# One transfer for w2 and one for dw2 in a decode block with its gradients: rows of 16.6 KB, one tile, a shared buffer for discarded results

## Chip, cores, metric

One Trainium2 chip, one core. The metric is the device time in microseconds of one execution, the median of several runs. Runs of two kernels are compared only when they were taken in the same rounds on the same chip.

## The reference, cut to what matters

The forward pass mixes an attention block with one query (A) and a small MLP (B) through a gate. The kernel computes the output and all gradients.

```python
g = sigmoid((x * gate_w).sum(-1))
a = A(x, k_cache, v_cache, wq, wo)     # 32 heads, 4096 keys, 128 wide: K and V are 33.6 MB each
b = B(x, w1, b1, w2)                   # h = x@w1 + b1; act = h*tanh(softplus(h)); act @ w2
out = g * a + (1 - g) * b
# outputs: out, dx, dK, dV, dwq, dwo, dw1, db1, dw2, dgate_w     (w2 is 1728 x 640, bf16)
```

K and V are read once and dK and dV are written once: 134 of the 165 MB that move. w2 is small beside this. Of its 1728 rows the first 1664 lie 13 to a partition: 13 x 640 x 2 B = 16640 B per partition.

## The kernel before

Heads are worked one after the other. In each, VectorE, PE and ScalarE pass small results to each other (row maximum, softmax, products); the two outer products dK and dV are VectorE's largest pieces. Loads go out on the sync queue (SP), most stores on GpSimd's (POOL). The MLP is cut into steps that are put into gaps ("slots") of the heads, at most four VectorE steps in a head.

```python
CH = [(0, 5), (5, 9), (9, FCN)]        # thirds of w2
def load_w2(c):
    a, b = CH[c][0], min(CH[c][1], FM)
    w2cs[c] = mlp.tile([P, 5, D], BF16, name="w2c", tag="w2c", bufs=2)     # two buffers for three thirds
    nc.sync.dma_start(w2cs[c][:, 0:b - a, :], w2_v[:, a:b, :])
...
load_k(2); load_v(2)
load_w2(0)
w2r = mlp.tile([FR, D], BF16, name="w2r", tag="w2r")
nc.sync.dma_start(w2r[:], B_w2[FB:F, :])
load_w2(1)
...
def dw2_part(c, f0, f1):               # dw2 is written in place over w2, then stored
    def f():
        for fc in range(f0, f1):
            r = rows(fc)
            nc.vector.tensor_scalar(w2p(fc), db_bc[0:r, :], m["act_f"][0:r, fc:fc + 1], None, ALU.mult)
        if f1 == CH[c][1]:
            a, b = CH[c][0], min(f1, FM)
            nc.gpsimd.dma_start(dw2_v[:, a:b, :], w2cs[c][:, 0:b - a, :])
...
# steps of third 2: four empty slots after the store of third 0, the load, eight empty slots, then its work
```

Steps `dh` (13 + 1 of them) and `dw2` belong to w2. `dxm` (10) and `dw1` (5) come after all `dh` steps. In each head the start is one instruction, the row maximum of the scores; I use it as the clock of the heads:

```python
def period(h):
    m32 = small.tile([P, 1], F32, name="m32", tag="m32")
    nc.vector.reduce_max(m32[:], S, axis=AX.X)
    ...
```

## Time and profile before

| | before |
|---|---|
| time, median of 3 runs | 402.32 us (402.15 to 402.79) |
| span of the profiled run | 400.8 us |
| bytes moved by DMA | 164.92 MB, 412 GB/s over the span |
| VectorE, PE busy | 76%, 75% |

A line of a stretch gives its length, the busy time of PE, weight load, VectorE, ScalarE and GpSimd with instruction counts, the granted clock, the share of time that the 16 DMA engines were busy (packets of two rings can overlap a little, so up to 1.03) and GB/s. The main reading of the page and the stretches is in the prediction below. Five further lines of the kernel before: from its chain of waits (start, length, what), the load of a K tile that compute waited for; from its stretches, the one that step 2 speaks of; from the view of the MLP tile, the steps after w2 (duration min/median/max, then first and last start); from the waits of the SP queue, a wait near the end (total us, times, longest):

```profile
49.57 33.56 DMA Kn<-in_A_k_cache_dram
```

```profile
168.00:174.00 6.00, 1.94 (x26) 1.10 (x25) 3.73 (x10) 0.58 (x1) 0.56 (x1) 0.71 1.02 421
```

```profile
L530 DVE SCALAR_TENSOR_TENSOR junk<-w_sb,dh_bc x10: 1040/1052/1059, 254.3 to 328.6; 128x864 bf16<-128x864 bf16 x10
L537 DVE TENSOR_SCALAR w_sb<-dh_bc,cols_f x5: 652/662/671, 274.1 to 332.4; 128x1728 bf16<-128x1728 bf16 x5
```

```profile
SPq L368 <- DMA out_dram<-dV_sb: 9.8, 1, 9.8
```

### The profile page before, as it was taken

To read this page: it belongs to the slowest core of one execution; us is meant where nothing else is said; L and a number is where in the kernel's file an instruction comes from. 1 tells how busy PE (TensorE), PEld (TensorE's weight loads), DVE (VectorE), ACT (ScalarE), POOL (GpSimd) and SP (SyncE) were. 2 spreads that over 40 slices of the span, in tenths; PEclk is the share of its full clock that TensorE was granted. 3 is DMA by queue.
4 is the path that set the end of the run, shared out by engine and by line. 5 is a ranking of instruction groups with operands and counts; after the bars stand their busy time and mean duration, and the time that the engine had idled before them with its cause. 6 is when DMAs were issued, how large, how long until landed. Compare 5 with 4: busy or idle time off the path is not lost.

```text
span 400.8 us, 13361 instructions
## 1 busy us (share of the span) xinstructions
PE 301.0 (75%) x5752; PEld 266.0 (66%) x5752; DVE 303.1 (76%) x783; ACT 178.2 (44%) x403; POOL 47.0 (12%) x94
## 2 busy tenths in 40 slices
PE   0788888678888788768879788838888888888300
PEld 0577888567777677658868778718777678877200
DVE  3339666556799999767658999836999997898860
ACT  1455454325545555326533555604545545555000
POOL 0001111021110111211110112101111121111000
PEclk9899999959999999969977999967999999999755
DMA  8999999999999999999999999999999999999995
GB/s 292 417 407 405 418 426 421 407 423 421 424 421 424 422 422 416 422 424 424 419 424 426 422 422 417 417 425 424 421 421 424 424 423 418 425 420 418 424 383 229
DMA packets 28359, 164.92 MB, mean 412 GB/s; under 512 B 3260, under 2 KB 3964, under 8 KB 12556
## 3 DMA queue, kind: packets, MB, share of 16 engines
q1 hardware_dynamic: 17136, 93.41, 56.5%
q0 software_dynamic: 11104, 70.64, 42.3%
q8 instruction: 45, 0.74, 0.7%
q14 instruction: 14, 0.11, 0.1%
q10 hardware_dynamic: 60, 0.01, 0.0%
HBM read 82.03 MB, written 82.03 MB: 409 GB/s over the span
## 4 chain that ended last, share of the span: by engine, by line
DVE 38%; DMA 32%; PE 20%; ACT 5%; issue 3%; ACTq 0%; SPq 0%
DMA Kn<-in_A_k_cache_dram 30%; DVE dK_sb L605 9%; DVE dV_sb L605 9%; PE tr L580 8%; DVE junk L378 5%; ACT tT L582 4%; DVE junk L278 3%; PE sA L660 3%; PE sA L589 3%; PE sB L713 3%; DVE junk L530 2%; DVE wo_g L367 1%; DMA vec_rows<-in_gate_w_dram 1%; DVE dj L700 1%; DVE dwq_t L732 1%
## 5 line engine op out<-in xcount | busy, mean ns | idle before, releaser
L582 ACT COPY tT<-tr 128x512 f32<-128x512 f32 x256 | 142.4, 587 | 127.8 <-PE tr L580 126.0
L589 PEld LDWEIGHTS <-tT 128*128 128x128 bf16 x2048 | 79.8, 98 | 40.3 <-ACT tT L582 34.6
L580 PE MATMUL tr<-ident_f,Kn 128*128 128x128 f32 x512 | 81.6, 297 | 9.2 <-DMA Kn<-in_A_k_cache_dram 9.2
L605 DVE TENSOR_TENSOR dV_sb<-p_bf,qd 128x2048 bf16<-128x2048 bf16 x64 | 78.0, 1218 | 0.2 <-issue 0.2
L605 DVE TENSOR_TENSOR dK_sb<-ds_bf,qd 128x2048 bf16<-128x2048 bf16 x64 | 77.7, 1216 | 0.0
L580 PE MATMUL tr<-ident_f,Vn 128*128 128x128 f32 x512 | 72.9, 278 | 0.0
L580 PEld LDWEIGHTS tr<-ident_f,Kn 128*128 128x128 f32 x512 | 61.0, 152 | 10.4 <-issue 10.4
L589 PE MATMUL sA<-qd,tT 128*128 128x48 bf16 x1024 | 48.7, 187 | 23.8 <-ACT dq_all L718 12.7
L580 PEld LDWEIGHTS tr<-ident_f,Vn 128*128 128x128 f32 x512 | 56.3, 142 | 0.0
L589 PE MATMUL sB<-qd,tT 128*128 128x48 bf16 x1024 | 46.0, 183 | 0.0
L660 PEld LDWEIGHTS <-Vn 128*128 128x128 bf16 x1024 | 30.2, 95 | 10.9 <-issue 10.9
L660 PE MATMUL sA<-e_bf,Vn 128*128 128x48 bf16 x1024 | 30.7, 183 | 8.1 <-DVE zs L680 6.5
L622 POOL DMA_DIRECT2D out_dram<-dK_sb x30 | 17.2, 574 | 138.9 <-DVE rz L682 86.5
L713 PE MATMUL sB<-ds_bf,Kn 128*128 128x48 bf16 x1024 | 32.2, 186 | 1.4 <-DVE ds_bf L702 1.4
L664 DVE TENSOR_REDUCE m<-sA 128x1 f32<-128x32 f32 x32 | 6.1, 189 | 32.9 <-PE sA L589 26.4
L713 PEld LDWEIGHTS <-Kn 128*128 128x128 bf16 x1024 | 29.5, 98 | 1.6 <-issue 1.6
L635 POOL DMA_DIRECT2D out_dram<-dV_sb x26 | 14.1, 542 | 135.8 <-DVE o_all L705 53.4
L278 DVE SCALAR_TENSOR_TENSOR junk<-wo_g,da_bc 128x640 bf16<-128x640 bf16 x32 | 26.2, 820 | 1.7 <-ACT da_bc L229 1.1
L378 DVE SCALAR_TENSOR_TENSOR junk<-wq_g,dq_bc 128x1024 bf16<-128x1024 bf16 (+1 forms) x25 | 25.1, 1005 | 0.2
L700 DVE TENSOR_SCALAR_CACHE_REDUCE dj<-sB,rz 128x128 f32<-128x128 f32 x32 | 11.1, 346 | 13.2 <-PE sB L694 13.2
L289 PE MATMUL q_ps<-wq_g,cols_bf 128*128 128x512 bf16 x40 | 13.1, 469 | 10.5 <-DMA wq_g<-in_A_wq_dram 10.5
L684 ACT ACTIVATE p_bf<-e_bf,rz 128x64 bf16<-128x64 bf16 x32 | 11.1, 348 | 13.9 <-DVE rz L682 11.1
(148 smaller groups left out, 268.8 us busy)
## 6 DMA issues: line engine op xcount, KB each, us to landing
Kn<-in_A_k_cache_dram SPq DMA_DIRECT2D x32, 1024.0 KB, 24.0
Vn<-in_A_v_cache_dram SPq DMA_DIRECT2D x32, 1024.0 KB, 28.0
out_dram<-dK_sb POOLq DMA_DIRECT2D x30, 1024.0 KB, 11.8
out_dram<-dV_sb POOLq DMA_DIRECT2D x26, 1024.0 KB, 11.8
wq_g<-in_A_wq_dram SPq DMA_DIRECT2D x4, 1280.0 KB, 23.2
wo_g<-in_A_wo_dram SPq DMA_DIRECT2D x8, 640.0 KB, 17.6
out_dram<-wo_g POOLq DMA_DIRECT2D x7, 640.0 KB, 11.8
out_dram<-dwq_t SPq DMA_DIRECT2D x4, 896.0 KB, 17.5
```

The lines of the kernel that those rows point to most:

```text
L278: nc.vector.scalar_tensor_tensor(junk[:, 0:D], in0=wos[g][:, i, :], scalar=1.0, in1=da_bc[:], op0=ALU.mult, op1=ALU.mult, accum_out=gp["do ...
L289: nc.tensor.matmul(q_ps[:], lhsT=x_bf[:, rc:rc + 1].to_broadcast([P, P]), rhs=wq[:, rc, off:off + GD], start=(rc == 0), stop=(rc == RC - 1))
L378: nc.vector.scalar_tensor_tensor(junk[:, c0:c1], in0=wqs[w][:, rc, c0:c1], scalar=1.0, in1=dq_bc[:, w * WG * Dh + c0:w * WG * Dh + c1], op ...
L580: nc.tensor.transpose(tp[:, t, :], flat[:, k * P:(k + 1) * P], ident_f[:])
L582: nc.scalar.copy(sb[:].rearrange("p a b -> p (a b)"), tp[:].rearrange("p a b -> p (a b)"))
L589: nc.tensor.matmul(out[:, 2 * k:2 * k + W], lhsT=tb[:, t, par, :], rhs=vec[:, par, :].unsqueeze(1).to_broadcast([P, W // 2, 2]), start=(pa ...
L605: nc.vector.tensor_tensor(dst[:, a:b, :].rearrange("p j (a b) -> p j a b", b=2), col[:, a:b, :].unsqueeze(2).to_broadcast([P, n, Dh // 2, 2]),
L622: ring(h).dma_start(dKv[h], st["dK"][:])
L635: ring(h).dma_start(dVv[h], st["dV"][:])
L660: nc.tensor.matmul(O, lhsT=vts[h][:, j, :], rhs=st["e"][:, j:j + 1].to_broadcast([P, W]), start=(j == 0), stop=(j == J - 1))
L700: nc.vector.tensor_scalar(dj[:], PT, rz[:], None, ALU.mult, ALU.add, accum_out=dd[:])
L713: nc.tensor.matmul(DQ, lhsT=kts[h][:, j, :], rhs=ds[:, j, 0:1].to_broadcast([P, W]), start=(j == 0), stop=(j == J - 1))
```

## The change

The intent is fewer and longer transfers for w2 and dw2, and no wait of the third chunk for a free buffer. w2 now has a tile of its own of 16640 B per partition in place of two buffers of 6400 B. Two discarded VectorE results (`pj`, `dj`) move into the junk buffer, so they need no tiles of their own (640 B per partition).

```diff
-    def load_w2(c):
-        a, b = CH[c][0], min(CH[c][1], FM)
-        w2cs[c] = mlp.tile([P, 5, D], BF16, name="w2c", tag="w2c", bufs=2)
-        nc.sync.dma_start(w2cs[c][:, 0:b - a, :], w2_v[:, a:b, :])
+    w2_all = mlp.tile([P, FM, D], BF16, name="w2_all", tag="w2_all")
+    for c in range(NCH):
+        w2cs[c] = w2_all[:, CH[c][0]:min(CH[c][1], FM), :]
 ...
-    load_w2(0)
+    nc.sync.dma_start(w2_all[:], w2_v)
     w2r = mlp.tile([FR, D], BF16, name="w2r", tag="w2r")
     nc.sync.dma_start(w2r[:], B_w2[FB:F, :])
-    load_w2(1)
 ...
-                    nc.gpsimd.dma_start(dw2_v[:, a:b, :], w2cs[c][:, 0:b - a, :])
                     if f1 == FCN:
+                        nc.gpsimd.dma_start(dw2_v, w2_all[:])
                         nc.gpsimd.dma_start(out_8[FB:F, :], w2r[:])
 ...
-            if c < 2:
-                done[f"w2_{c}"] = -1
-            else:
-                (4 empty steps, the load of the third chunk, 8 empty steps)
+            done[f"w2_{c}"] = -1
 ...
-        pj = small.tile([P, J], F32, name="pj", tag="pj", bufs=1)
+        pj = f32v(junk[:])[:, 0:J]
 ...
-        dj = small.tile([P, P], F32, name="dj", tag="dj", bufs=1)
+        dj = f32v(junk[:])[:, 0:P]
```

More of the change, by code (lines that the diff above doesn't have):

```diff
@@ L497, in f @@
                 if f1 == CH[c][1]:
-                    a, b = CH[c][0], min(f1, FM)
-                    nc.gpsimd.dma_start(dw2_v[:, a:b, :], w2cs[c][:, 0:b - a, :])
                     if f1 == FCN:
+                        nc.gpsimd.dma_start(dw2_v, w2_all[:])
                         nc.gpsimd.dma_start(out_8[FB:F, :], w2r[:])
@@ L553, in mlp_steps @@
             add(f"dw2_{c}", "D", dw2_part(c, a + 3, b), (f"dw2a_{c}",), H0)
-            if c < 2:
-                done[f"w2_{c}"] = -1
-            else:
-                for k in range(4):
-                    add(f"w2w{k}_{c}", "T", lambda: None, (f"w2w{k - 1}_{c}" if k else f"dw2_{c - 2}",), H0)
-                add(f"w2l_{c}", "T", lambda c=c: load_w2(c), (f"w2w3_{c}",), H0)
-                for k in range(8):
-                    last = k == 7
-                    add(f"w2_{c}" if last else f"w2x{k}_{c}", "T", lambda: None,
-                        (f"w2x{k - 1}_{c}" if k else f"w2l_{c}",), H0)
+            done[f"w2_{c}"] = -1
         add("dhc", "T", dh_cast, (f"dh_{FCN - 1}",), H0)
@@ L689, in period @@
         part = small.tile([P, 1], F32, name="part", tag="part")
-        pj = small.tile([P, J], F32, name="pj", tag="pj", bufs=1)
-        nc.vector.scalar_tensor_tensor(pj[:], in0=DP[:, 0:J], scalar=1.0, in1=e[:], op0=ALU.mult, op1=ALU.mult,
+        pj = f32v(junk[:])[:, 0:J]
+        nc.vector.scalar_tensor_tensor(pj, in0=DP[:, 0:J], scalar=1.0, in1=e[:], op0=ALU.mult, op1=ALU.mult,
                                        accum_out=part[:])
@@ L698, in period @@
         dd = small.tile([P, 1], F32, name="dd", tag="dd")
-        dj = small.tile([P, P], F32, name="dj", tag="dj", bufs=1)
-        nc.vector.tensor_scalar(dj[:], PT, rz[:], None, ALU.mult, ALU.add, accum_out=dd[:])
+        dj = f32v(junk[:])[:, 0:P]
+        nc.vector.tensor_scalar(dj, PT, rz[:], None, ALU.mult, ALU.add, accum_out=dd[:])
         ds = st["ds"] = small.tile([P, J, 2], BF16, name="ds_bf", tag="ds_bf")
```

## The prediction

> **What bounds the kernel now.** I read the slices of the page first, to see whether one resource is full from end to end; then stretches of the span with their DMA share; then the chain of waits; then the transfers and the waits of the queue that issues the loads. First the page:
>
> ```profile
> span 400.8 us, 13361 instructions
> PE 301.0 (75%) x5752; PEld 266.0 (66%) x5752; DVE 303.1 (76%) x783; ACT 178.2 (44%) x403; POOL 47.0 (12%) x94
> ...
> DMA  8999999999999999999999999999999999999995
> ...
> DMA packets 28359, 164.92 MB, mean 412 GB/s; under 512 B 3260, under 2 KB 3964, under 8 KB 12556
> ...
> DVE 38%; DMA 32%; PE 20%; ACT 5%; issue 3%; ACTq 0%; SPq 0%
> ```
>
> No compute engine passes 76%, but the DMA row is 9 in every slice but the first and the last. The chain of waits names VectorE first (38%). That is no proof of a VectorE bound: the chain follows the last instruction, and here the last thing to end is a transfer. The stretches settle it (columns: length, busy time of each engine, granted clock, DMA share, GB/s):
>
> ```profile
> 0.00:4.00 4.00, 0.00 (x0) 0.00 (x0) 1.45 (x7) 1.28 (x1) 0.99 (x12) 1.00 0.46 124
> 4.00:76.00 72.00, 57.39 (x1046) 50.49 (x1047) 42.94 (x122) 34.04 (x78) 5.59 (x11) 0.98 1.02 414
> 76.00:84.00 8.00, 3.85 (x30) 2.19 (x30) 3.88 (x12) 0.58 (x1) 0.10 (x1) 0.65 1.02 412
> 84.00:168.00 84.00, 71.25 (x1438) 64.08 (x1437) 73.13 (x196) 42.95 (x99) 12.93 (x24) 0.97 1.01 421
> ...
> 260.00:270.00 10.00, 3.56 (x44) 1.80 (x40) 3.02 (x11) 0.59 (x1) 0.00 (x0) 0.64 1.02 424
> 270.00:388.00 118.00, 89.53 (x1779) 79.94 (x1779) 106.57 (x262) 53.35 (x122) 14.54 (x24) 0.92 1.01 422
> 388.00:401.00 13.00, 0.00 (x0) 0.00 (x0) 0.00 (x0) 0.17 (x1) 0.00 (x0) 0.50 0.60 237
> ```
>
> The DMA share is 1.0 from 4 to 388 us, whether compute is hungry (76:84 and 260:270, where PE is under half busy and waits for K) or is itself the chain (270:388, VectorE 106.6 of 118 us). The rate is 412 to 424 GB/s in both. From 388 on no engine computes and stores drain for 12 us. A longer look at the records of the single packets gives their price: 309 ns for 8192 B and 159 ns for 4096 B (medians), so about 9 ns plus 36.6 ns per KB (1000 B); 6400 B took 244, 5120 B 196. All packet times over 16 engines sum to 399.3 us of a 400.8 us span. So bytes and packets on the 16 engines are the bound.
>
> The tail is not a compute tail either. The semaphore counts of the last stores show that the 16 shares land in two groups: of the last half of dK, five landed by 388.2 us and the last at 396.5; of the final one (dwq_l) six by 395.2, the last at 399.7. The late group had work queued without a break until 399.7. The slowest DMA engine ends the kernel.
>
> **What the Trainium skill says.**
> - "DMA: Bandwidth & Descriptors", section "Issuing engines are not separate DMA queues": transfers of all issuing engines run on the same 16 and interleave. The trace agrees: the SP and POOL rings carry 93.4 and 70.6 MB, and the rate stays at 422 GB/s when the mix of compute changes. So moving w2 in time moves other transfers and doesn't add or remove work.
> - Same page, "Why small descriptors are slow (HBM only)": a fixed cost per packet of about 3 cycles. The trace has such a constant, 9 ns; at 5 to 6 KB it is under 5%.
> - Same page, "Rules for kernel authors": coalesce, since transfers under 64 KB are mostly overhead. The w2 pieces have 640 and 800 KB, far above; and the fixed latency is hidden behind a full queue, as the share of 1.0 shows.
> - "DVE: scalar operands, raw-bit mode, write accounting and state across instructions": the DVE queue is one in-order queue. So sharing one junk buffer among VectorE instructions needs no wait. The trace can't show that before the change; its junk writers have no waits for each other now.
>
> **The change, part by part.** The transfers it touches:
>
> ```profile
> w2c<-in_B_w_dram SPq DMA_DIRECT2D x2, 640.0 KB
> out_dram<-w2c POOLq DMA_DIRECT2D x2, 640.0 KB, 14.0
> ...
> w2c<-in_B_w_dram SPq DMA_DIRECT2D x1, 800.0 KB, 18.5
> out_dram<-w2c POOLq DMA_DIRECT2D x1, 800.0 KB, 11.3
> ```
>
> 1. Packets. Each partition row of w2 goes now as 6400 + 5120 + 5120 B = 244 + 196 + 196 = 636 ns, after as one of 16640 B = 9 + 609 = 618 ns (if it stays one packet). 18 ns x 128 rows x 2 directions / 16 engines = 0.29 us. Four transfers fewer save four completion packets of 9 ns on each engine: 0.04 us. Sum -0.33 us on the resource that binds. Bytes unchanged.
>
> 2. The third w2 chunk (655 kB) is loaded at about 16 us, not at 164. It now stands ahead of the K and V loads of the early heads: 0.655 MB / 0.42 MB per us = 1.6 us later for what follows, until 164 us, where the old load is gone and everything is level again. The K tile whose landing ends the first hunger (issued at 49.57, landed at 83.1 us) should land near 84.5. PE starves 1.6 us longer there and 1.6 us less near 168. Net on the DMA path: 0.
>
> 3. Semaphores of the SP queue. A transfer waits for the landing of the one 8 earlier in the rotation (it shows as a wait for an unrelated tile). The load of K for head 3 waits now for w1:
>
> ```profile
> SPq L121 <- DMA w_sb<-in_B_w_dram: 5.1, 1, 5.1
> ```
>
> With one w2 load less ahead of it, it waits for wo instead, which has landed by 20.4 us, so it issues about 5 us earlier, at 20.5. The ring had work all through, so this only lengthens the queue: 0. The last stores keep their distance of 8 in the rotation, so the wait of 9.8 us of the last dwo store for a dV store stays.
>
> 4. The MLP steps. Twelve empty steps that delayed the third chunk fall away. I filled VectorE's step slots by hand (up to four a head, by priority): dh and dw2 of the third chunk move from 226-249 us into nearly empty slots of the heads from 180 to 205, and the dxm/dw1 steps (1.05 + 0.08 and 0.66 us) begin near 226 in place of 254 and end near 280 in place of 332. Some 8 steps, about 8 us of VectorE, leave the stretch 270:388. That would pay if VectorE set the end; it doesn't, the DMA share there is already 1.01. Compute runs into K waits instead. The dw1 store is tied to a head (338.6 us) and doesn't move. Net 0, at best a few tenths in the tail.
>
> 5. The dw2 stores at 152.9, 183.7 and 249.2 become one at about 205 us. 1.66 MB at once on the POOL ring holds the dV/dK stores behind it for 2 to 4 us. Output buffers: 5, two used per 10 us head, stores land in 11.8 us (median), so about 25 - 12 = 13 us of slack: no wait.
>
> 6. pj and dj into junk: same instructions, same shapes: 0.
>
> Sum: 402.32 - 0.33 = 402.0; a little for the tail, so 401.9.
>
> **Rivals.**
> - Compute bounds the last third, as the chain says (VectorE without a DMA step from 276 us on). Then step 4 is worth something: 8 us of VectorE less, and the tail fills better. Five engines idle up to 8.3 us at the end, 5/16 x 8.3 = 2.6 us of average capacity, so at most about 399.3. Against: DMA share 1.01, and the late engines had no break.
> - The long burst hurts. A 16.6 KB packet holds an engine for 618 ns, twice an 8 KB one; the early delay of step 2 might not be paid back if compute catches up too late; or the big store delays output buffers after all. For: compute is itself close to the bound (VectorE 90% in 270:388). Each would cost 1 to 2 us: 403.5 to 404.
> - Long rows run faster or slower than the line through 4 and 8 KB says. At 10% either way: 2 x 128 x 618 / 16 = 9.9 us of engine time, so 1 us either way.
> - A new dependency: with w2 in one tile, in-place dw2 writes to one chunk might be ordered against PE's reads of another. PE would wait for at most a few 0.38 us instructions, hidden under DMA: 0.
>
> **Range and chances.** Working sum 401.9. Down: a better tail, at most -2.6, of which I allow half: 400.4. Up: 1.5 us of unreturned delay: 403.4. Two per cent would be 8 us; nothing in the working reaches that: the w2 traffic in all is 3.3 of 164.9 MB, 8 us of DMA time, and it stays. Chances: faster 0.015, same 0.965, slower 0.02.
>
> **What would show it right or wrong.** Right: DMA row 9 throughout; w2 once in and once out, 1664 KB, packets down by some 512 row and 64 completion packets to about 27,780; first PE hunger later by about 1.6 us; dxm/dw1 ended near 280; VectorE in 270:388 lower by about 8 us at the same rate of 422 GB/s, with K waits returning there; last stores landing in two groups, at about 399. Wrong: a DMA share below 1 in mid-span, VectorE waiting on output buffers after 205 us, w2 rows split into more packets, or an end that came earlier by more than 2 us with the same bytes (then compute did bind the last third).

## The result, and the profile after

| | before | after |
|---|---|---|
| time, median of 6 runs each | 402.31 us (402.08 to 402.79) | 403.08 us (401.82 to 403.76) |
| span of the profiled run | 400.8 us | 402.0 us |
| DMA packets | 28359 | 27783 |
| VectorE busy, 270 to 388 us | 106.57 us | 98.54 us |

The ratio is 1.0013, with a 95% interval of 0.9994 to 1.0032: the same. Ratios here are the mean time of one kernel's fast runs over that of the other's of the same rounds, so not quite the ratio of the medians quoted. The profiled run after was the slowest of its six (403.76 us); its span says more about scatter than about the change. Two further sets of runs of the changed kernel are told below. Over all three sets it took 402.73 us on average (16 runs) and the kernel before 402.52 us (24 runs of the same rounds).

The page after, lines that answer to those of before:

```profile
span 402.0 us, 13373 instructions
DMA  8999999999999999999999999999999999999984
DMA packets 27783, 164.91 MB, mean 410 GB/s; under 512 B 3196, under 2 KB 3900, under 8 KB 11724
DVE 37%; DMA 27%; PE 23%; ACT 7%; issue 3%; ACTq 0%; SPq 0%; DVEq 0%
```

The bytes are the same, 576 packets are gone, and the DMA row is full as before. The stretches after:

```profile
168.00:174.00 6.00, 3.71 (x65) 2.63 (x61) 5.79 (x16) 1.45 (x3) 0.66 (x2) 1.00 1.02 422
270.00:388.00 118.00, 89.89 (x1779) 80.62 (x1779) 98.54 (x246) 53.37 (x122) 14.26 (x24) 0.90 1.01 420
388.00:402.00 14.00, 0.00 (x0) 0.00 (x0) 0.00 (x0) 0.00 (x0) 0.00 (x0) 0.50 0.55 219
```

From 270 to 388 us VectorE has 8.0 us less to do, and the DMA engines are as full as before (1.01), at 420 GB/s where it was 422. The w2 transfers, the steps after them, the K tile and the SP waits after:

```profile
w_all<-in_B_w_dram SPq DMA_DIRECT2D x1, 2080.0 KB
out_dram<-w_all POOLq DMA_DIRECT2D x1, 2080.0 KB, 19.0
```

```profile
L527 DVE SCALAR_TENSOR_TENSOR junk<-w_sb,dh_bc x10: 1040/1050/1059, 202.4 to 280.5; 128x864 bf16<-128x864 bf16 x10
L534 DVE TENSOR_SCALAR w_sb<-dh_bc,cols_f x5: 660/662/671, 231.0 to 284.9; 128x1728 bf16<-128x1728 bf16 x5
```

```profile
49.91 34.37 DMA Kn<-in_A_k_cache_dram
```

```profile
SPq L366 <- DMA out_dram<-dV_sb: 8.7, 1, 8.7
SPq L126 <- DMA w_sb<-in_B_w_dram: 5.1, 1, 5.1
SPq L121 <- DMA wo_g<-in_A_wo_dram: 1.0, 1, 1.0
```

The MLP steps end 47 us earlier (284.9 against 332.4). The K tile lands at 84.3 us against 83.1. The wait for w1 (`w_sb`) passed from the K load of head 3 (L121) to the V load behind it (L126). Each of these moved as foreseen, and the end did not.

The single packets, from the trace's own records (medians, and the sum of all packet times over 16 engines):

```
                     before       after
8192 B               309 ns       309 ns
5120 B               196 ns       196 ns
6400 B, w2           244-247 ns   none
16640 B, w2 and dw2  none         620 ns stored, 623 ns loaded
sum / 16             399.3 us     399.1 us
```

A row of 16640 B is one packet, and its price lies on the line through the smaller ones (9 + 16640 x 0.0366 = 618 ns).

### The profile page after: what moved, and what is told of

Same layout as the page of the kernel before. It is cut to its first block, busy times and chain, and to the rows that moved or that the text cites. A ratio compares the mean times of both kernels' runs of the same rounds, so it can differ in the third digit from the quotient of the medians.

```text
span 402.0 us, 13373 instructions
## 1 busy us (share of the span) xinstructions
PE 299.7 (75%) x5752; PEld 263.5 (66%) x5752; DVE 303.7 (76%) x783; ACT 178.2 (44%) x403; POOL 46.0 (11%) x92
## 2 busy tenths in 40 slices
DMA packets 27783, 164.91 MB, mean 410 GB/s; under 512 B 3196, under 2 KB 3900, under 8 KB 11724
## 4 chain that ended last, share of the span: by engine, by line
DVE 37%; DMA 27%; PE 23%; ACT 7%; issue 3%; ACTq 0%; SPq 0%; DVEq 0%
DMA Kn<-in_A_k_cache_dram 21%; DVE dK_sb L593 9%; PE tr L568 8%; DVE dV_sb L593 8%; ACT tT L570 6%; DVE junk L376 4%; DMA Vn<-in_A_v_cache_dram 4%; PE sA L648 4%; PE sA L577 3%; DVE junk L276 3%; PE sB L701 3%; DVE wo_g L365 1%; DMA vec_rows<-in_gate_w_dram 1%; DVE junk L485 1%; DVE junk L688 1%
## 5 line engine op out<-in xcount | busy, mean ns | idle before, releaser
L568 PE MATMUL tr<-ident_f,Kn 128*128 128x128 f32 x512 | 79.2, 290 | 5.2 <-DMA Kn<-in_A_k_cache_dram 5.1
L593 DVE TENSOR_TENSOR dK_sb<-ds_bf,qd 128x2048 bf16<-128x2048 bf16 x64 | 77.8, 1216 | 0.0
L568 PEld LDWEIGHTS tr<-ident_f,Kn 128*128 128x128 f32 x512 | 58.7, 148 | 6.7 <-issue 5.7
L701 PEld LDWEIGHTS <-Kn 128*128 128x128 bf16 x1024 | 29.7, 98 | 1.9 <-issue 1.9
L688 DVE TENSOR_SCALAR_CACHE_REDUCE junk<-sB,rz 128x128 f32<-128x128 f32 x32 | 11.1, 346 | 14.0 <-PE sB L682 14.0
```

Of the source, the lines that this page charges most:

```text
L568: nc.tensor.transpose(tp[:, t, :], flat[:, k * P:(k + 1) * P], ident_f[:])
L593: nc.vector.tensor_tensor(dst[:, a:b, :].rearrange("p j (a b) -> p j a b", b=2), col[:, a:b, :].unsqueeze(2).to_broadcast([P, n, Dh // 2, 2]),
L688: nc.vector.tensor_scalar(dj, PT, rz[:], None, ALU.mult, ALU.add, accum_out=dd[:])
L701: nc.tensor.matmul(DQ, lhsT=kts[h][:, j, :], rhs=ds[:, j, 0:1].to_broadcast([P, W]), start=(j == 0), stop=(j == J - 1))
```

## The experiments

All gave correct results but one.

### e1: the changed kernel again

No edit.

> The changed kernel again, unchanged. Theory S (scatter of one DMA engine): the six runs fell into two clusters, 401.8-402.0 and 403.0-403.8, and in the profiled one (403.76) one engine's share of every late store landed 1.7 us after the other fifteen. If that straggler is what makes the slow cluster, the new runs fall into the same two clusters, and the lag of the last share in the new profile is about 1.7 us when its time is above 403, and below 0.5 us when it is near 402. Rival F (a fixed cost of about 1 us in the change): all runs near 403.1, whatever the lag.

Measured: 402.28 us (402.06, 402.13, 402.28, 402.80, 402.89) against 402.43; ratio 1.0001 (0.9988 to 1.0013). The rival of a fixed cost of 1 us falls. The theory of two clusters isn't borne out either: five runs without a gap, and in the profiled one (402.28) the last share of the last dK store landed 0.8 us after the fifteenth, neither 1.7 nor under 0.5.

### e2: three stores

```diff
+                    a, b = CH[c][0], min(f1, FM)
+                    nc.gpsimd.dma_start(dw2_v[:, a:b, :], w2_all[:, a:b, :])
                     if f1 == FCN:
-                        nc.gpsimd.dma_start(dw2_v, w2_all[:])
```

> The changed kernel, but dw2 stored in three pieces as each third is done, so only the load is whole. Theory S and packets: 256 packets more than the changed kernel, 256 x 9 ns / 16 = 0.14 us more engine time, same time within 0.5 us. Rival B (the burst of the whole store delays the tail): 0.5 to 1 us faster than the changed kernel, and without its slow cluster.

Measured: 403.46 us (402.84 to 403.62), ratio to before 1.0024 (1.0011 to 1.0036), 1.2 us above e1 by medians. A miss for both theories. The rival (the burst of the whole store delays the tail) has the wrong sign. It was repeated as e12. The packet records say where the profiled run of e2 (403.62 us) lost time: packets that start from 248 to 260 us and from 276 to 284 us took together 1.2 us per engine more than the median of their size, where those of e12 took 0.3. The last w2 transfer was issued at 200.0 us and landed within some 16, so neither stretch holds one; why packets are slow there is open.

### e3: whole transfers, old order of the steps

```diff
-            done[f"w2_{c}"] = -1
+            if c < 2:
+                done[f"w2_{c}"] = -1
+            else:
+                for k in range(13):       # 12 empty steps, then "w2_2" counts as there
+                    add(..., lambda: None, ...)
```

> The changed kernel with the 12 empty steps of the old kernel put back ahead of the third chunk: whole transfers, old order of the MLP steps. DMA bound: same time within 0.5 us, although VectorE has about 8 us more in the stretch from 270 to 388 us. Rival C (VectorE bounds the last third): slower than the changed kernel by 3 us or more. Rival F2 (the earlier MLP steps cost the changed kernel 1 us): faster by 0.8 us, at about 402.0.

Measured: 402.20 us (401.94 to 402.45), ratio to before 0.9995 (0.9982 to 1.0009), 0.1 us below e1. Its stretch, and that of e1:

```profile
270.00:388.00 118.00, 88.90 (x1778) 79.19 (x1777) 106.19 (x262) 53.54 (x122) 14.55 (x24) 0.92 1.01 421
```

```profile
270.00:388.00 118.00, 87.54 (x1778) 78.42 (x1776) 98.30 (x245) 53.33 (x122) 14.27 (x24) 0.92 1.01 421
```

VectorE 106.2 against 98.3 us, the same 421 GB/s, the same time. VectorE's busy time in the last third is not what sets the end.

### e4: the same bytes in short rows

```diff
-    nc.sync.dma_start(w2_all[:], w2_v)
+    nc.sync.dma_start(w2_all[:], w2_v, max_dma_last_dim=1280)
-    nc.gpsimd.dma_start(dw2_v, w2_all[:])
+    nc.gpsimd.dma_start(dw2_v, w2_all[:], max_dma_last_dim=1280)
```

> The changed kernel with the w2 load and the dw2 store cut into rows of 1280 B, 13 packets per partition in place of 1. Packet theory: 12 x 128 x 2 x 9 ns / 16 = 1.7 us more on the engines, so about 1.7 us slower than the changed kernel (404.5 to 405). Rival: packet overhead is hidden by the other ring's traffic: same time within 0.5 us.

Measured: 404.51 us (403.87 to 404.65), 2.2 us above e1; packets are not hidden. The working behind the expectation was wrong, though. The load came in 1664 packets of 1280 B, as meant, but the dw2 store in 416 of 5120 B, not 1664. By the means in the trace the load cost 1664 x 59.3 ns / 16 = 6.2 us in place of 128 x 627 ns / 16 = 5.0, and the store 416 x 198.7 / 16 = 5.2 in place of 5.0: together 1.3 us. The sum of all packet times over 16 engines rose by more, from 398.8 in e1 to 401.6 us, since other packets took longer too. Of that other 1.4 us, 0.8 can be placed: packets that start from 248 to 256 us, long after both w2 transfers, took 1.0 us per engine more than the median of their size, and 0.2 in e1. Why is open, and so is how much of the 2.2 us is due to the shorter rows beyond the 1.3 that the packets of these two transfers show.

### e5: without the dw2 store

```diff
                     if f1 == FCN:
-                        nc.gpsimd.dma_start(dw2_v, w2_all[:])
```

> The changed kernel without the whole dw2 store, so that output is wrong on purpose. 1.66 MB less of 164.9. DMA bound: 128 x 620 ns / 16 = 5.0 us of engine time less, so about 4 to 5 us faster (398). Rival C (the compute chain sets the end): less than 1 us faster, since no compute instruction is gone.

Measured: 397.16 us against 402.55 before; ratio 0.9862 (0.9848 to 0.9877), 5.4 us faster. Only the output dw2 was wrong. (The expectation says 1.66 MB; it is 2.13 MB, a slip of mine that runs through the prediction too. The 5.0 us beside it came from the packets and was right.) No compute instruction is gone, and the time fell by about what the transfer took (5.0 us by its packets). This is the clearest sign of what binds.

### e6 and e7: more VectorE work in the kernel before

```diff
         nc.vector.reduce_max(m32[:], S, axis=AX.X)
+        if 22 <= h < 30:
+            for _ in range(2):        # 6 in e7
+                nc.vector.tensor_scalar(junk[:, 0:1024], dq_bc[:, 0:1024], x_f[:, 0:1], None, ALU.mult)
```

> The kernel before with two extra VectorE instructions (128x1024, about 0.4 us each) in each of the heads 22 to 29: 6.4 us of VectorE in the stretch where the chain of waits names VectorE. Rival C (VectorE sets the end there): 4 to 6 us slower. DMA bound: the last dV store waits 15 us in its queue anyway, so same time within 1 us, with the tail's stores issued up to 6 us later.

> The same with six extra instructions a head: 19 us of VectorE. Now both theories expect a loss; they differ in its size. Rival C: 15 to 19 us slower. DMA bound with about 15 us of queued stores as slack plus some idle VectorE time (11 us in that stretch): 0 to 6 us slower.

Measured: e6 403.30 us, 0.75 us above its 402.55 before (ratio 1.0013, 0.9996 to 1.0029). e7 424.77 us, 22.2 us above (ratio 1.0551). e6 is as the DMA bound says. e7 is outside of both expectations, so I looked at the clock of the heads. Starts of head 22 and head 31 before, of head 31 in e6, and in e7 (view: VectorE's instructions in order of time; in brackets the idle time before):

```profile
277.77 0.19 DVE L664 TENSOR_REDUCE m<-sA 128x1 f32<-128x32 f32 x1 [3.01 <-PE sA L589]
...
367.31 0.19 DVE L664 TENSOR_REDUCE m<-sA 128x1 f32<-128x32 f32 x1 [0.92 <-PE sA L589]
```

```profile
373.66 0.19 DVE L664 TENSOR_REDUCE m<-sA 128x1 f32<-128x32 f32 x1 [0.91 <-PE sA L589]
```

```profile
396.99 0.19 DVE L664 TENSOR_REDUCE m<-sA 128x1 f32<-128x32 f32 x1 [0.92 <-PE sA L589]
```

In e6 compute is 6.4 us late at head 31 and the end 0.75 us. In e7 compute is 29.7 us late, more than the 23.3 us of added work, and the end 22.2. So some 6 to 8 us of delay are free (an estimate: the differences 5.6 and 7.5 us, from one profile each), and after that each microsecond counts. The added instructions lie in front of the head's softmax, where each head's other engines wait for them, so the heads stretched from 9.2 to 11.8 us to 12.4 to 16.3. The stretch of e7 shows the DMA engines running dry, which of all kernels here only e7 and e10 do in mid-span:

```profile
L667 DVE TENSOR_SCALAR junk<-dq_bc,cols_f x48: 477/486/492, 277.3 to 376.0; 128x1024 bf16<-128x1024 bf16 x48
```

```profile
280.00:380.00 100.00, 68.32 (x1237) 61.47 (x1236) 89.19 (x206) 39.23 (x88) 10.30 (x18) 0.89 0.89 345
```

A share of 0.89 and 345 GB/s: loads and stores were not asked for fast enough. VectorE is busy 89.2 of 100 us here, no more than before (106.57 of 118, 90%). It is the length of the dependency chain of a head that grew. Why by more than the added work isn't settled: the granted clock from 280 to 380 us was also lower, 0.89 in e7 and 0.98 before, and no run separates the two.

### e8: pj and dj alone

The kernel before with the last two hunks of the change (`pj`, `dj`) and nothing else.

> The kernel before with pj and dj put into the shared junk buffer and nothing else. In-order VectorE, same shapes: same time within 0.3 us, no new wait. Rival: the shared buffer makes VectorE wait for itself: 64 instructions x some 0.1 us, 1 us or more slower if on the path, and visible as idle time before dj and pj in any case.

Measured: 402.38 us against 402.55, ratio 0.9995 (0.998 to 1.001). The groups before and in e8 (busy, mean ns; then idle time before them and its cause):

```profile
L700 DVE TENSOR_SCALAR_CACHE_REDUCE dj<-sB,rz 128x128 f32<-128x128 f32 x32 | 11.1, 346 | 13.2 <-PE sB L694 13.2
```

```profile
L700 DVE TENSOR_SCALAR_CACHE_REDUCE junk<-sB,rz 128x128 f32<-128x128 f32 x32 | 11.0, 345 | 14.2 <-PE sB L694 14.2
```

346 against 345 ns, and the wait is for PE in both. No instruction waits for the shared buffer. This part costs nothing.

### e9 and e10: the same extra work in the changed kernel

The edit of e6 and e7, put into the changed kernel.

> The changed kernel with the same two extra VectorE instructions in the heads 22 to 29 (16 x 0.486 us = 7.8 us). The kernel before took 0.75 us from them. Theory L (the change bought 8 us of VectorE slack in the last third, which the full DMA engines can't turn into time): within 0.5 us of the changed kernel. Rival N (no slack was bought): 0.7 us or more slower than the changed kernel.

> The changed kernel with six extra instructions a head (23.3 us), which cost the kernel before 22.2 us. Theory L: the slack of about 8 us is used up first, so 12 to 16 us slower. Rival N: about 22 us slower, as before.

Measured: e9 402.88 us, 0.2 us above the changed kernel (e11, 402.71). That is what theory L said, but 0.75 and 0.2 us are both within the scatter of these kernels. e10 425.12 us, 22.4 us above e11: theory L falls. The change did not buy 8 us of slack. The clock of the heads says how much it bought: head 31 of the changed kernel starts at

```profile
366.06 0.19 DVE L652 TENSOR_REDUCE m<-sA 128x1 f32<-128x32 f32 x1 [0.91 <-PE sA L577]
```

that is 1.25 us earlier than before (367.31), for 8 us of VectorE less. One profile isn't enough here: in e1 and in e11 it starts at

```profile
363.75 0.19 DVE L652 TENSOR_REDUCE m<-sA 128x1 f32<-128x32 f32 x1 [0.92 <-PE sA L577]
```

```profile
364.68 0.19 DVE L652 TENSOR_REDUCE m<-sA 128x1 f32<-128x32 f32 x1 [0.92 <-PE sA L577]
```

3.6 and 2.6 us earlier than before, because head 22, too, starts at another time in each run (277.77 before; 277.45, 275.13 and 276.09 in these three). From head 22 to head 31 all three need 88.6 us, and the kernel before 89.5: in that stretch the 8 us of VectorE were worth 0.9. Heads 22 and 23 became 0.6 us shorter each (10.0 and 9.8 us to 9.4 and 9.2); heads of 9.2 us were there before, and no head got below that. In the other heads the removed steps had lain in idle time of VectorE. So compute, too, was not bound by VectorE's sum but by a head's chain of some 9.2 us. e10 says the same: its stretch has VectorE busy 77.8 us where e7 had 89.2, and the two kernels take about the same time (425.12 and 424.77 us).

```profile
280.00:380.00 100.00, 71.42 (x1204) 64.39 (x1204) 77.82 (x184) 38.45 (x87) 9.54 (x17) 0.81 0.89 345
```

### e11 and e12: changed kernel and three stores once more

> The changed kernel a third time. The two earlier sets had medians of 403.1 (6 runs, 401.8 to 403.8) and 402.3 (5 runs, 402.1 to 402.9). If the spread is that of the last DMA engine and not a cost, the median is again between 402 and 403.1 with single runs between 401.8 and 403.8; no clusters are expected any more.

> The version with three dw2 stores a second time; it took 403.5 against 402.3 for the changed kernel in the same rounds, which 0.14 us of packets don't explain. If it was chance, it is now within 0.5 us of the changed kernel of this call. If it is a property of this version, it is again about 1 us slower.

Measured: e11 402.71 us (402.48 to 403.35), ratio 1.0006 (0.9992 to 1.0020). e12 402.93 us (402.47 to 403.30), ratio 1.0005 (0.9993 to 1.0018). The changed kernel lies where expected. The loss of e2 did not come back: 0.2 us above e11, against 1.2 above e1. Differences of 1 us between sets of five runs of these kernels aren't to be believed, although the interval of e2 alone excluded 1.

No experiment pointed to a version better than both kernels. None undercut the kernel before by more than its scatter but e5, which leaves out an output.

## Why the prediction was right

It said 401.9 us (400.4 to 403.4) and "same"; 403.1 was measured, within the range but in its upper part, and 402.7 over all 16 runs. "Same" was safe whatever became of the 0.33 us, since two per cent are 8 us; what the runs confirm is the bound, not that term. (Half of 2.6 us below 401.9 is 400.6; the 400.4 of the range is a slip.) By its own steps:

- **The bound.** Right, and tested: e5 took away one transfer of 2.13 MB and no compute instruction and got 5.4 us; e3 moved 8 us of VectorE and got nothing; e6 added 7.8 us of VectorE (16 x 0.486) and lost 0.75. What it did not see is how near the second bound lies: a head's dependency chain, with 6 to 8 us of slack at head 31 (e6 and e7).
- **Step 1, packets.** The count was 27783 (said: about 27,780), a row one packet of 620 ns (said: 618). The sum of packet times fell by 0.25 us in the profiled run, by 0.5 in e1 and by 1.0 in e11 (said: 0.33); it scatters by 0.7 us among profiles of one kernel, so this doesn't measure the term. In the time it can't be seen either: the runs of the changed kernel spread over 1.9 us. e4 shows that packets aren't hidden, with a larger size.
- **Sizes.** "1664 KB" and "1.66 MB" are wrong: 16640 B x 128 partitions is 2080 KB or 2.13 MB, and the w2 traffic in all is 4.26 MB, not 3.3, about 10 us of DMA time. Step 5's "2 to 4 us" leans on the wrong size: at 420 GB/s the store is about 5 us. The steps that carry the sum used rows and packets and are untouched.
- **Step 2, the early load.** The K tile landed 1.2 us later (said: 1.4). Near 168 us PE starved less: 3.71 us busy between 168 and 174 where it was 1.94. Given back as said.
- **Step 3, semaphores.** The wait of 5.1 us for w1 moved to the next load; the K load issued at 20.5 us as said. The wait of the last dwo store stayed (9.8, now 8.7 us).
- **Step 4, MLP steps.** The last dw1 started at 284.9 us (said: near 280), dxm began at 202 (said: 226; one step found an earlier slot), VectorE fell by 8.0 us in 270:388 (said: 8). K waits did not return there, which the prediction had counted among the signs of being right; this step failed: PE waited for K once between 270 and 390 us before (1.9 us) and once after (1.2 us), both at 270 us. Compute hardly got ahead, so there was little to wait for (I take this for the reason; no run tests it). The first rival, "compute bounds the last third", gave too much for VectorE's busy time: the 8 us were worth 0.9 us of head time from head 22 to head 31.
- **Step 5, the burst.** No wait for an output buffer followed the store at 197.3 us, whose landing took 19.0 us. A single one of 1.2 us came at 247.7 us, some 50 us later, and a wait of this kind after 205 us is among the prediction's own signs of being wrong; it shows in all three profiles of the changed kernel, and not in those of the kernel before, e3, and the two runs with three stores. It is also there in e4 (0.7 us) and missing in e5, which has no dw2 store; but it is missing in e9 and e10, too, whose code is that of the changed kernel up to head 22. So the whole store may have a part in it and doesn't bring it every time; its cause stays open, and so whether the end noticed.
- **Step 6, junk.** Confirmed alone by e8. The page on the DVE that the prediction names says "one in-order queue" in its section "Flops that outlive an instruction"; e8 agrees, since the groups that it shows kept their 346 ns and waited for PE alone.
- **The tail.** Two groups of DMA engines end apart, as before; the last share of all landed at 400.8 us in the profiled run after and at 399.3 in e1 (said: about 399). In the profiled run after (403.76 us) one engine's share of the last dK store landed 1.7 us after the fifteenth; in e1 it was 0.8, in the kernel before 0.14. A late last engine goes with a late end there, but over all runs it isn't a clean law (0.5 us in e12 at 402.93 us, 0.95 in e2 at 403.62; and e2 had slow packets besides), and why one engine falls behind in one run and not in the next stays open. So does whether the changed kernel's wider spread (0.58 us standard deviation over 16 runs, 0.25 over 24 before) is a property of it.

## What to carry to other kernels

A chain of waits that ends in compute doesn't prove that compute sets the time: look at the DMA share of the same stretch, and test by taking bytes away and by adding work. Coalescing transfers that are already hundreds of kilobytes, behind a queue that never runs empty, saves only the packets' constants: here 576 x 9 ns over 16 engines. And when steps leave a busy engine, ask for the length of the dependency chain of one iteration before counting them as a gain.

## What the Trainium skill lacked or had wrong

- "DMA: Bandwidth & Descriptors", section "Where 436 GB/s comes from": it says that for transfers between HBM and SBUF the HBM side of about 358 GB/s binds. Here one core moved 420 GB/s, reads and writes together, from 4 to 388 us. A note beside the page's table of measurements keeps the 358 to the case that both cores of a pair stream, which this sentence doesn't; here one core ran, and the 425 that the section quotes fits better. Its section on small descriptors gives the constant per packet in cycles only (by the table stands one figure, about 10.5 ns, from a 4 KB transfer); here it is 9 ns a packet, on a line through 159, 309 and 620 ns for 4096, 8192 and 16640 B.
- The same page, section "SWDGE vs HWDGE vs iDMA", gives a packet as preferably at most 4096 B. The trace of the changed kernel records 16640 B as one packet on both rings, at 620 and 623 ns. A store cut into rows of 1280 B was recorded as 416 packets of 5120 B, the load cut alike as 1664 of 1280 B. That a packet may hold several descriptors is on the page; no page says that the two issuing paths pack such rows differently.
- No page says how far apart the engines end after a long full run; there is only a remark that two of the 16 are usually slower, and one that a bulk load goes at the pace of its slowest engine. In the kernel before, five of the 16 shares of the last dK store landed by 388.2 us and the slowest at 396.5; of the very last store six landed by 395.2 and the slowest at 399.7.
